# The last chunk's attention due between the preceding chunk's MLP steps, and the block products' bank copies all by ScalarE, ahead of its other work

## The chip, the cores and the metric

The kernel runs on one core of one Trainium2 chip. A core has five engines that run side by side, each taking its own instructions strictly in order: TensorE (PE: matrix products; PEld is its weight load), VectorE (DVE), ScalarE (ACT), GpSimd (POOL) and SyncE (SP), which here issues every DMA. Matrix products land in PSUM banks, which VectorE and ScalarE can read. The metric is the device time of one execution in microseconds, median of three runs.

## The reference, cut to what matters

Attention with a window of 32 positions (half of the heads take every fourth of 128 positions) over 4 batches, 8 heads, 576 positions, head size 64, and then two gated MLPs over the 2304 x 512 result, all in fp32:

```python
x = attn_out.transpose(0, 2, 1, 3).reshape(2304, 512)
xn = x / sqrt(mean(x * x) + 1e-6) * rms_g
x = (silu(xn @ w_gate) * (xn @ w_val)) @ w_out          # 512 -> 1536 -> 512
y = (sigmoid(x @ w2_gate) * (x @ w2_val)) @ w2_out      # 512 -> 1536 -> 512
```

## The kernel before, in words

**Number format.** Every fp32 operand of a product is split into a high and a low half (`split`: the high half by ScalarE or VectorE at L402 or L404, the low half by GpSimd or VectorE at L406 or L409), and a product takes three matmuls: high by high, high by low, low by high. Weights arrive as 64-bit words; `words` turns each block of 128 x 512 of them into fp32 with one ScalarE instruction (L380) and four on VectorE (L386, L389, L392, L395). Such a block is called a word here. `weight_ahead` makes words ahead of time, stores them to DRAM, and the second MLP's 36 words are made so while the first MLP runs. Each word takes one of three SBUF buffers named `wst`, filled by a DMA, and holds it until its L395.

**Stages.** 48 attention groups (`attn_group`: scores L700, masks L711, exponentials L717, transposes L742, values L754, each group a chain through PE, VectorE, ScalarE, VectorE, GpSimd, PE, ScalarE, PE, ScalarE) give the input of six chunks of 384 tokens. `x_norm` takes a chunk's root mean square (squares L798, sums over blocks L806 by GpSimd, over partitions L814 by PE), a Newton iteration on tiny tiles (L848 to L852, GpSimd), spreads and transposes the factor (L855, L870) and writes the split operands `xo`. The first MLP runs over the six chunks twice, with half of its hidden width each time: 72 steps (`mlp_step` and `y_group`), each a gate product (L973, bank g), a value product (L973, bank v), tanh and two multiplications (L985, L987, L991), the split into `h`, and the four output products of the step before it (L1010). Steps 0 to 35 take chunks 0 to 5, six steps each, so chunk 5 begins at step 30, and its `x_norm` must be done by then.

**Second MLP.** It runs over pairs of chunks of 288 tokens in `unit`, with seven block products in place of eight (L1147), sums of blocks being made beforehand (`weight_blocks` L485, `x_blocks` L926, whose seven split operands lie in buffers named xo, wst and xo2). A unit takes the seven products into three banks: X (bank g or v), and Z and Y (both named att). Three times a bank is copied out (`snap`, L1157 on ScalarE or L1159 on VectorE), so that the next product can be added to the same bank or a later result can be made from the copy; VectorE adds the other banks to these copies (`plus`, L1164). There are 24 units of two such halves, 48 x 3 = 144 copies. The next product to a copied bank waits for the copy.

**What sets the order.** All instructions are handed to `Line`, with a cost, a due time and the data they need. `emit` walks a planned clock: on each engine it takes the operation that can start first, and of several that can start at the same time the one with the smallest due time. An operation with `other=` may go to a second engine, which counts as starting later by a penalty of PARAMS. The result is a fixed order on each engine. Due times of attention groups come from pairs lo and hi, on a clock where step k of the first MLP is due at 6.24 k:

```python
lo, hi = PARAMS[f"lo{c}"], PARAMS[f"hi{c}"]
for i, g in enumerate(span):
    due[g] = lo + (hi - lo) * i / len(span)
```

The second MLP's words have a release time on the planned clock (`t + 135` in `whole`), before which `emit` doesn't take them.

Of the kernel before, what the change touches and what calls it, by code (L numbers as in the profile page):

```python
# [23 lines left out]

PARAMS = {
    "margin": 187.0, "wait": 0.344, "w_sq": 2.0, "w_hi": 0.6, "w_lo": 0.6, "x_hi": 0.5, "x_lo": 0.5,
    "h_hi": 0.3, "h_lo": 0.5, "qk": 0.2, "norm": 4.0, "pts": 4.0, "o": 2.0, "snap": 0.4, "ys": 1.0,
    "ts": 1.0, "cross": 0.25, "same": 0.064, "dma_lat": 2.0, "dma_rate": 260e3,
# [3 lines left out]
    "wdue": -7.2, "wslope": 2.65, "wload": -378.6, "wload_step": 37.9,  # L32
    "warm_n": 18, "warm_t": 10.103, "warm_dt": 0.322, "warm_c": 19, "warm_m": 5, "warm_late": 0.218,
    "warm_due": 15.435, "mask_cost": 0.224, "exp_cost": 0.387, "s_cost": 0.8, "o_cost": 0.6,
# [31 lines left out]
class Line:  # L66
# [13 lines left out]
    def add(self, eng, cost, fn, reads=(), writes=(), tiles=(), due=0.0, lat=0.0,  # L80
            release=0.0, until=None, other=(), bus=0.0):

        o = Op()
        o.ways = {eng: (cost, fn, 0.0)}
        if other:
            kind, eng, cost, fn = other
            o.ways[eng] = cost, fn, PARAMS[kind]  # L90
        o.eng, o.tiles, o.due, o.lat = None, list(tiles), due, lat
        o.seq, o.succs, o.end, o.release = len(self.ops), [], None, release
        o.until, o.bus = until, bus
        preds = set()
        for key in reads:
            if key not in self.writer:
                raise KeyError(key)
            preds.add(self.writer[key])
            self.readers.setdefault(key, []).append(o)
        for key in writes:  # L100
            if key in self.writer:
                preds.add(self.writer[key])
            preds.update(self.readers.pop(key, ()))
            self.writer[key] = o
        preds.discard(o)
        o.preds, o.left = preds, len(preds)
        for p in preds:
            p.succs.append(o)
        for t in o.tiles:
            t.users += 1  # L110
        self.ops.append(o)
        return o
# [78 lines left out]
def attention_then_two_gated_mlps(  # L191
# [15 lines left out]
    nc = tc.nc  # L207
# [7 lines left out]
    T = S // 2  # L215
# [58 lines left out]
    def act(n):  # L274
        return 0.17 + n / 1200

    def dve(n):
        return 0.155 + n / 960
# [847 lines left out]
    def unit(p, b, u, at, extra):  # L1126
# [5 lines left out]
        for which in range(2):  # L1132
            uk = (p, b, u, which)
# [3 lines left out]
            ck = {name: ("c", name, uk) for name in c}  # L1137
# [17 lines left out]
            def snap(name, bank, key):  # L1155
                t = c[name]
                add("ACT", act(T), lambda: nc.scalar.copy(out=t.t, in_=bank.t),  # L1157
                    reads=[(key, uk)], writes=[ck[name]], tiles=[bank, t], due=at,
                    other=("snap", "DVE", dve(T), lambda: nc.vector.tensor_copy(  # L1159
                        out=t.t, in_=bank.t)))  # L1160

            def plus(name, bank, key):
                t = c[name]
# [4 lines left out]
            def finish(name):  # L1168
# [3 lines left out]
                if which == 0:  # L1172
# [13 lines left out]
                      ("hs", p, 2 * b + half, f + e), [tk], [], [t], at, "h")  # L1186

            steps = (("X", lambda: snap("11", X, "X")),
                     ("Z", lambda: (plus("11", Z, "Z"), finish("11"))),
                     ("X", lambda: snap("12", X, "X")),  # L1190
                     ("Y", lambda: snap("22", Y, "Y")),
                     ("X", lambda: (plus("22", X, "X"), finish("22"))),
                     ("Y", lambda: (plus("12", Y, "Y"), finish("12"))),
# [207 lines left out]
```

## Time and profile before

| what | before |
|---|---|
| median of 3 runs (lowest to highest) | 1080.74 us (1080.61 to 1081.27) |
| the profiled execution | 1078.51 us, of which 1076.7 us are the span of the trace |
| busy: PE, DVE, ACT, POOL | 1006.9, 695.7, 458.0, 503.7 us |
| mean granted clock of TensorE | 0.969 |
| first MLP's steps 0 to 71 | about 128 to 624 us of the span |
| second MLP | about 628 to 1077 us |

A row of the trace's timeline has the start, the duration, the engine, the line, what is written from what, and in brackets the idle time of that engine just before with the instruction that ended it. The granted clock is 1.00 when TensorE runs at 2.4 GHz and 0.5 when it runs at 1.2 GHz.

### The profile page before, as it was taken

How to read it: one execution, taken by the hardware profiler on the slowest of the kernel's cores; microseconds unless marked ns; L12 is line 12 of the kernel's file. 1: busy time of each engine (PE TensorE's matmuls, PEld its weight loads, DVE VectorE, ACT ScalarE, POOL GpSimd, SP SyncE). 2: the span in 40 equal slices, each digit the busy share in tenths (PEclk: the TensorE clock that was granted, in tenths of full speed). 3: DMA queues.
4: the chain of work that ended last, by engine and by line, in shares of the span. 5: the costliest groups of instructions: out<-in, count | busy, mean ns of one | idle time of the engine just before them, and what ended most of it. 6: DMA issues, size and time to landing. Idle time of an engine off the chain costs nothing.

```text
span 1076.7 us, 20044 instructions
## 1 busy us (share of the span) xinstructions
PE 1006.9 (94%) x7254; PEld 964.7 (90%) x7254; DVE 695.7 (65%) x1479; ACT 458.0 (43%) x1231; POOL 503.7 (47%) x659
## 2 busy tenths in 40 slices
PE   5989699989997799999999988999999999999997
PEld 4768588879996799999999978999999999999996
DVE  3699967686551326777777987647554666466733
ACT  4867655554332233322223344445544344433321
POOL 3476956454322444512213765438553466553511
PEclk8779899999998799999999999999999999999999
DMA  7858468783440635866765641213323332334334
GB/s 159 177 170 180 117 173 189 166 218 107 155 137 30 208 116 190 299 202 212 265 227 176 192 136 44 69 43 102 108 72 126 110 130 86 116 99 105 72 80 89
DMA packets 190899, 152.05 MB, mean 141 GB/s; under 512 B 131376, under 2 KB 163120, under 8 KB 190800
## 3 DMA queue, kind: packets, MB, share of 16 engines
q1 hardware_dynamic: 190800, 150.77, 48.1%
q8 instruction: 57, 0.93, 0.4%
q14 instruction: 42, 0.34, 0.1%
HBM read 103.55 MB, written 47.19 MB: 140 GB/s over the span
## 4 chain that ended last, share of the span: by engine, by line
PE 71%; DVE 12%; DMA 4%; SPq 4%; issue 4%; POOL 3%; ACT 2%; DVEq 0%; POOLq 0%; ACTq 0%
PE y L1010 23%; PE g L973 12%; PE v L973 11%; PE att L1147 9%; PE g L1147 6%; PE v L1147 5%; SPq L612 1%; PE att L700 1%; DVE t L1180 1%; SPq L659 1%; PE att L754 1%; DVE h L404 1%; DVE wz L389 1%; DMA wst<-in_moe_w_val_dram 1%; DVE h L409 1%
## 5 line engine op out<-in xcount | busy, mean ns | idle before, releaser
L1010 PE MATMUL y<-h,wo 128*128 128x288 f32 (+1 forms) x2016 | 369.9, 313 | 2.0 <-POOL h L406 1.0
L1010 PEld LDWEIGHTS y<-h,wo 128*128 128x128 f32 x2016 | 318.5, 188 | 4.6 <-POOL h L406 1.6
L406 POOL TENSOR_TENSOR h<-t,h 128x288 fp32r<-128x288 f32 (+1 forms) x149 | 146.1, 983 | 303.8 <-ACT h L402 238.9
L973 PE MATMUL g<-xo,w 128*128 128x384 f32 x864 | 170.8, 345 | 5.5 <-DVE t L987 2.5
L973 PE MATMUL v<-xo,w 128*128 128x384 f32 x864 | 163.8, 337 | 0.0
L973 PEld LDWEIGHTS g<-xo,w 128*128 128x128 f32 x864 | 154.2, 193 | 10.0 <-DVE t L987 3.2
L973 PEld LDWEIGHTS v<-xo,w 128*128 128x128 f32 x864 | 150.4, 188 | 1.5
L402 ACT CAST h<-t 128x288 fp32r<-128x288 f32 (+1 forms) x140 | 65.6, 471 | 139.7 <-DVE t L991 76.1
L730 POOL TENSOR_SCALAR pr<-pr,rs 128x96 f32<-128x96 f32 x144 | 63.6, 457 | 79.9 <-DVE rs L725 52.3
L1147 PE MATMUL att<-xo,w 128*128 128x288 f32 x576 | 92.7, 296 | 0.8
L985 ACT ACTIVATE t<-g 128x384 f32<-128x384 f32 x72 | 35.4, 491 | 121.8 <-PE g L973 121.7
L1164 DVE TENSOR_TENSOR t<-t,att 128x288 f32<-128x288 f32 x96 | 43.4, 452 | 65.3 <-PE att L1147 61.6
L1147 PEld LDWEIGHTS att<-xo,w 128*128 128x128 f32 x576 | 81.4, 188 | 2.2 <-DVE t L1159 2.2
L987 DVE SCALAR_TENSOR_TENSOR t<-t,g 128x384 f32<-128x384 f32 x72 | 39.7, 551 | 67.2 <-ACT t L985 66.9
L406 POOL TENSOR_TENSOR xo<-xq,xo 128x576 fp32r<-128x576 f32 x36 | 53.9, 1506 | 35.0 <-ACT xo L402 35.0
L392 DVE SCALAR_TENSOR_TENSOR wz<-wst,wz 128x512 int32<-128x512 int32 x72 | 67.7, 940 | 1.4
L1147 PE MATMUL v<-xo,w 128*128 128x288 f32 x396 | 64.1, 297 | 2.9 <-DVE t L1159 2.8
L380 ACT ACTIVATE wz<-wst 128x512 f32<-128x512 f32 x72 | 48.1, 668 | 39.3 <-DMA wst<-in_moe_w_gate_dram 17.4
L717 ACT ACTIVATE pr<-pr,nmx 128x96 f32<-128x96 f32 x144 | 52.6, 367 | 28.5 <-DVE nmx L711 28.3
L1147 PE MATMUL g<-xo,w 128*128 128x288 f32 x396 | 63.2, 295 | 0.0
L991 DVE TENSOR_TENSOR t<-t,v 128x384 f32<-128x384 f32 x72 | 39.6, 550 | 34.0 <-PE v L973 33.5
L395 DVE SCALAR_TENSOR_TENSOR wz<-wst,wz 128x512 int32<-128x512 int32 x72 | 60.5, 840 | 1.5
(170 smaller groups left out, 1597.5 us busy)
## 6 DMA issues: line engine op xcount, KB each, us to landing
z<-wz SPq DMA_DIRECT2D x54, 256.0 KB
wst<-in_moe_w_gate_dram SPq DMA_DIRECT2D x24, 512.0 KB
wst<-in_moe_w_val_dram SPq DMA_DIRECT2D x24, 512.0 KB
wst<-in_moe_w_out_dram SPq DMA_DIRECT2D x24, 512.0 KB
z<-z SPq DMA_DIRECT2D x48, 256.0 KB
xq<-y SPq DMA_DIRECT2D x20, 576.0 KB
x<-xo SPq DMA_DIRECT2D x12, 768.0 KB
xo<-x SPq DMA_DIRECT2D x12, 768.0 KB
```

The costliest lines, as they stand in the source:

```text
L380: add("ACT", act(CW), lambda: nc.scalar.activation(out=z.t.bitcast(F32), in_=top().bitcast(F32), func=ACTF.Square), reads=[("wst", key)], ...
L392: add("DVE", dve(CW), lambda: nc.vector.scalar_tensor_tensor(out=z.t, in0=top(), scalar=-0x40000000, in1=z.t, op0=ALU.bitwise_and, op1=ALU ...
L395: add("DVE", dve(CW), lambda: nc.vector.scalar_tensor_tensor(out=z.t, in0=low(), scalar=29, in1=z.t, op0=ALU.logical_shift_right, op1=ALU. ...
L402: add("ACT", act(n), lambda: nc.scalar.copy(out=hi(), in_=src()), reads=reads, writes=[key] + [order] * bool(order), tiles=tiles + [dst], ...
L406: add("PL", pool(n), lambda: nc.gpsimd.tensor_tensor(out=lo(), in0=src(), in1=hi().bitcast(F32), op=ALU.subtract), reads=reads, writes=[ke ...
L717: add("ACT", PARAMS["exp_cost"], lambda u=u: nc.scalar.activation(out=pr.t[:, u], in_=pr.t[:, u], func=ACTF.Exp, bias=nmx.t[:, u:u + 1], s ...
L730: add("PL", 0.33, lambda u=u: nc.gpsimd.tensor_scalar(out=pr.t[:, u], in0=pr.t[:, u], scalar1=rs.t[:, u:u + 1], scalar2=1.0, op0=ALU.mult, ...
L973: nc.tensor.matmul(out=bank.t, lhsT=w[:, l, cols], rhs=x[:, r, j], start=kk == 0 and n == 0, stop=kk == KD - 1 and n == 2)
L987: add("DVE", dve(T1), lambda: nc.vector.scalar_tensor_tensor(out=t.t, in0=t.t, scalar=1.0, in1=gb.t, op0=ALU.add, op1=ALU.mult), writes=[k ...
L1010: nc.tensor.matmul(out=yb.t, lhsT=w.t[:, l, s], rhs=h.t[:, r], start=n == 0 and j == 0, stop=n == nf - 1 and j == 2)
L1147: nc.tensor.matmul(out=bank.t, lhsT=l.t[:, a, cols], rhs=r.t[:, d, j], start=first and j == 0 and m == 0, stop=j == 1 and m == 2, skip_gro ...
L1164: add("DVE", dve(T), lambda: nc.vector.tensor_tensor(out=t.t, in0=t.t, in1=bank.t, op=ALU.add), reads=[(key, uk)], writes=[ck[name]], tile ...
```

## The change

The span of due times of the last chunk's attention groups goes from 186.7 falling to 113.2, to 80.0 rising to 140.0. The bank copies of `snap` lose their second engine, and their due time falls by 150.

```diff
-    "h_hi": 0.3, "h_lo": 0.5, "qk": 0.2, "norm": 4.0, "pts": 4.0, "o": 2.0, "snap": 0.4, "ys": 1.0,
+    "h_hi": 0.3, "h_lo": 0.5, "qk": 0.2, "norm": 4.0, "pts": 4.0, "o": 2.0, "snap": 150.0, "ys": 1.0,
...
-    "hi4": 108.9, "lo5": 186.7, "hi5": 113.2, "lead": -15.1, "xdue": 7.2,
+    "hi4": 108.9, "lo5": 80.0, "hi5": 140.0, "lead": -15.1, "xdue": 7.2,
...
             def snap(name, bank, key):
                 t = c[name]
                 add("ACT", act(T), lambda: nc.scalar.copy(out=t.t, in_=bank.t),
-                    reads=[(key, uk)], writes=[ck[name]], tiles=[bank, t], due=at,
-                    other=("snap", "DVE", dve(T), lambda: nc.vector.tensor_copy(
-                        out=t.t, in_=bank.t)))
+                    reads=[(key, uk)], writes=[ck[name]], tiles=[bank, t],
+                    due=at - PARAMS["snap"])
```

Three places of the resulting order follow. A row names the line, the operation, the written tile and what is read, and the free size. Lines behind L1159 have one number less in the changed kernel.

**TensorE, steps 28 to 30.** Before, between step 28's output products and step 30's gate product stand the last attention group (L700, L742, L754) and chunk 5's sums (L814) and transpose (L870):

```order
L973 MATMUL g<-xo,w 128x384 x12
L973 MATMUL v<-xo,w 128x384 x12
L1010 MATMUL y_4261<-h,wo 128x384 x3
L1010 MATMUL y_4269<-h,wo 128x384 x3
L1010 MATMUL y_4274<-h,wo 128x384 x3
L1010 MATMUL y_4279<-h,wo 128x384 x3
L700 MATMUL att<-kT,qT 64x96 x6
L742 MATMUL att<-ident,pr 96x128 x3
L754 MATMUL att<-pts,v 64x64 x6
L814 MATMUL att<-ones,pt 128x1 x3
L870 MATMUL att<-ident,rb 128x128 x3
L973 MATMUL g<-xo,w 128x384 x12
```

In the changed kernel the L700 to L754 rows of the last groups stand at steps 15 to 21, L814 behind step 22's value product and L870 among the output products behind step 23's, and at steps 29 and 30 there are MLP products alone. Step 15, which had the scores of two groups before, has those of four in the changed kernel (the row x12 holds two):

```order
L973 MATMUL v<-xo,w 128x384 x12
L754 MATMUL att<-pts,v 64x64 x6
L700 MATMUL att<-kT,qT 64x96 x12
L1010 MATMUL y_3223<-h,wo 128x384 x3
L1010 MATMUL y_3232<-h,wo 128x384 x3
L700 MATMUL att<-kT,qT 64x96 x6
L1010 MATMUL y_3276<-h,wo 128x384 x3
L1010 MATMUL y_3298<-h,wo 128x384 x3
L700 MATMUL att<-kT,qT 64x96 x6
L973 MATMUL g<-xo,w 128x384 x12
L742 MATMUL att<-ident,pr 96x128 x6
```

What moved: nothing of attention or of chunk 5's norm is left ahead of step 30.

**VectorE, from the first MLP's end to the first bank sum of the second MLP.** Before (L485 sums weight blocks, L409 and L404 split, L1033 takes the first MLP's last outputs, L1164 is the first unit's first `plus`):

```order
L485 TENSOR_TENSOR S_7193<-z_7093,z_7144 128x256
L485 TENSOR_TENSOR S_7200<-S_7185,z_7093 128x256
L409 TENSOR_TENSOR xo_7187<-xq_5905,xo_7187 128x576
L409 TENSOR_TENSOR wst_7202<-T3_5968,wst_7202 128x576
L404 CAST wo_7219<-z_7177 128x512
L1033 SCALAR_TENSOR_TENSOR pt_6624<-y0_6902,pt_6624 128x384
L1033 SCALAR_TENSOR_TENSOR pt_6624<-y1_6908,pt_6624 128x384
L1033 SCALAR_TENSOR_TENSOR pt_6624<-y2_6913,pt_6624 128x384
L1033 SCALAR_TENSOR_TENSOR pt_6624<-y3_6922,pt_6624 128x384
L409 TENSOR_TENSOR w_7211<-S_7185,w_7211 128x256
L485 TENSOR_TENSOR S_7257<-z_7093,S_7200 128x256
L1164 TENSOR_TENSOR t_7252<-t_7252,att_7245 128x288
```

In the changed kernel:

```order
L392 SCALAR_TENSOR_TENSOR wz_7182<-wst_7113,wz_7182 128x512
L1033 SCALAR_TENSOR_TENSOR pt_6588<-y0_6866,pt_6588 128x384
L395 SCALAR_TENSOR_TENSOR wz_7182<-wst_7113,wz_7182 128x512
L485 TENSOR_TENSOR S_7245<-z_7066,S_7197 128x256
L386 TENSOR_SCALAR wz_7235<-wz_7235 128x512
L1033 SCALAR_TENSOR_TENSOR pt_6588<-y1_6871,pt_6588 128x384
L389 SCALAR_TENSOR_TENSOR wz_7235<-wst_7170,wz_7235 128x512
L1033 SCALAR_TENSOR_TENSOR pt_6588<-y2_6876,pt_6588 128x384
L392 SCALAR_TENSOR_TENSOR wz_7235<-wst_7170,wz_7235 128x512
L1033 SCALAR_TENSOR_TENSOR pt_6588<-y3_6885,pt_6588 128x384
L395 SCALAR_TENSOR_TENSOR wz_7235<-wst_7170,wz_7235 128x512
L1163 TENSOR_TENSOR t_7233<-t_7233,att_7224 128x288
```

What moved: before, the last word's L395 stands in step 69; in the changed kernel two of the four words behind step 69 are made between the last step's products and the first bank sum. The first unit's sixth and seventh products read the operands wst_7264 and wst_7295, which take over the buffers of wst_7113 and wst_7170.

**VectorE, one later unit.** Before, three copies (L1159) of one half unit stand among the sums (L1164), the gates (L1180) and a split:

```order
L1159 COPY t2_8289<-v_8267 128x288
L1164 TENSOR_TENSOR t2_8289<-t2_8289,att_8282 128x288
L1180 SCALAR_TENSOR_TENSOR t2_8214<-t2_8214,t2_8289 128x288
L404 CAST h2_8322<-t2_8214 128x288
L1159 COPY t2_8324<-v_8267 128x288
L409 TENSOR_TENSOR h2_8322<-t2_8214,h2_8322 128x288
L1159 COPY t2_8340<-att_8315 128x288
L1164 TENSOR_TENSOR t2_8340<-t2_8340,v_8267 128x288
```

In the changed kernel:

```order
L1163 TENSOR_TENSOR t2_8280<-t2_8280,att_8282 128x288
L1179 SCALAR_TENSOR_TENSOR t2_8214<-t2_8214,t2_8280 128x288
L404 CAST h2_8319<-t2_8214 128x288
L409 TENSOR_TENSOR h2_8319<-t2_8214,h2_8319 128x288
L409 TENSOR_TENSOR wst_8324<-xq_8026,wst_8324 128x576
L1163 TENSOR_TENSOR t2_8330<-t2_8330,v_8267 128x288
```

What moved: the copies are all on ScalarE, 144 rows of L1157 where there were 115, and a low half (wst_8324) stands among VectorE's rows.

## Rows read from the trace of the kernel before

**Rows 1.** The page, part 1: busy time, share of the span, instructions.

```profile
PE 1006.9 (94%) x7254; PEld 964.7 (90%) x7254; DVE 695.7 (65%) x1479; ACT 458.0 (43%) x1231; POOL 503.7 (47%) x659
```

**Rows 2.** Five stretches: length, busy time of each engine, PE clock, DMA share, GB/s.

```profile
140.00:335.00 195.00, 189.88 (x1465) 174.79 (x1464) 125.71 (x343) 89.02 (x282) 82.96 (x155) 1.00 0.58 155
335.00:365.00 30.00, 15.63 (x82) 13.05 (x81) 7.74 (x21) 7.11 (x20) 9.88 (x22) 0.66 0.31 103
365.00:620.00 255.00, 253.86 (x1462) 252.90 (x1461) 177.84 (x269) 80.16 (x166) 96.48 (x92) 1.00 0.63 209
620.00:660.00 40.00, 32.44 (x213) 30.24 (x212) 35.54 (x52) 20.02 (x46) 27.81 (x23) 1.00 0.28 90
660.00:1060.00 400.00, 393.77 (x2943) 389.35 (x2942) 238.52 (x442) 167.76 (x399) 195.91 (x193) 1.00 0.31 93
```

**Rows 3.** PE's waits from 335 to 365 us: total, times, longest.

```profile
PE att L870 <- DVE rb L855: 4.7, 1, 4.7
PE att L814 <- POOL pt L806: 4.6, 1, 4.6
```

**Rows 4.** PE's timeline, output products of steps 27, 28 and 29.

```profile
330.93 2.24 PE L1010 MATMUL y<-h,wo 128*128 128x384 f32 x12
...
337.17 2.25 PE L1010 MATMUL y<-h,wo 128*128 128x384 f32 x12
...
365.79 2.24 PE L1010 MATMUL y<-h,wo 128*128 128x384 f32 x12
```

**Rows 5.** PE's timeline, steps that hold parts of attention or norm.

```profile
257.51 2.24 PE L973 MATMUL g<-xo,w 128*128 128x384 f32 x12
...
271.11 2.24 PE L973 MATMUL g<-xo,w 128*128 128x384 f32 x12
...
275.26 2.24 PE L1010 MATMUL y<-h,wo 128*128 128x384 f32 x12
...
289.55 2.35 PE L1010 MATMUL y<-h,wo 128*128 128x384 f32 x12
```

**Rows 6.** PE's waits from 620 to 660 us.

```profile
PE g L1147 <- DVE t L1159: 3.1, 1, 3.1
PE att L1147 <- DVE t L1159: 1.9, 1, 1.9
```

**Rows 7.** PE's waits from 660 to 1060 us.

```profile
PE v L1147 <- DVE t L1159: 4.4, 7, 1.6
...
PE g L1147 <- ACT t L1157: 0.4, 1, 0.4
```

**Rows 8.** The bank copies, largest group of each engine: ns least/median/most, first and last start.

```profile
L1157 ACT COPY t<-g x46: 378/400/402, 629.6 to 1040.6; 128x288 f32<-128x288 f32 x46
...
L1159 DVE COPY t<-v x18: 443/455/459, 638.6 to 1014.7; 128x288 f32<-128x288 f32 x18
```

**Rows 9.** VectorE's instructions of a word, by line: busy us, mean ns.

```profile
L392 DVE SCALAR_TENSOR_TENSOR wz<-wst,wz 128x512 int32<-128x512 int32 x72 | 67.7, 940 | 1.4
L395 DVE SCALAR_TENSOR_TENSOR wz<-wst,wz 128x512 int32<-128x512 int32 x72 | 60.5, 840 | 1.5
L389 DVE SCALAR_TENSOR_TENSOR wz<-wst,wz 128x512 int32<-128x512 int32 x72 | 58.0, 805 | 1.9
...
L386 DVE TENSOR_SCALAR wz<-wz 128x512 f32<-128x512 f32 x72 | 41.9, 582 | 24.9 <-ACT wz L380 24.7
```

**Rows 10.** Timeline at the second MLP's start: last outputs, first bank sum, seventh product.

```profile
623.61 2.42 PE L1010 MATMUL y<-h,wo 128*128 128x384 f32 x13
...
634.20 0.44 DVE L1164 TENSOR_TENSOR t<-t,att 128x288 f32<-128x288 f32 x1
...
636.75 1.05 PE L1147 MATMUL g<-wst,w 128*128 128x288 f32 x6
```

**Rows 11.** Timeline of VectorE, one instruction of a word beside GpSimd's and one apart.

```profile
602.49 1.54 DVE L389 SCALAR_TENSOR_TENSOR wz<-wst,wz 128x512 int32<-128x512 int32 x1
...
613.53 0.69 DVE L389 SCALAR_TENSOR_TENSOR wz<-wst,wz 128x512 int32<-128x512 int32 x1
```

## The prediction, written before the changed kernel ran

> **What bounds the kernel now.** The page's first part comes first: PE is busy for 94% of the span and no other engine for more than 65% [rows 1]. So time can only come from the stretches in which PE stands still or runs at the lower clock. The stretches show them [rows 2]. From 140 to 335 us PE idles 5.1 us, from 365 to 620 us 1.1, from 660 to 1060 us 6.2. From 335 to 365 us it is busy for 15.6 of 30 us, with a granted clock of 0.66, so it spends part of that stretch at 1.2 GHz. From 620 to 660 us it idles 7.6 us while VectorE is busy for 35.5 of 40. The kernel is thus bound by PE except in two places: step 29 of the first MLP, and the start of the second MLP. In the first, the waits name the chain of the last chunk's norm: 4.6 us for GpSimd's sums of squares and 4.7 us for the spread factor behind the Newton iteration [rows 3], each once, with nothing else for PE to do. In the second, VectorE's queue is the cause: the longest waits are for bank copies that stand in it [rows 6]. From 660 us on the same copies cost 4.4 of 6.2 us, seven times [rows 7].
>
> **The hole at step 29.** The change takes attention and norm out of step 29 and puts them between steps 15 and 23. A plain step is 6.24 us, from 330.93 to 337.17; the next output products start at 365.79, so two steps took 34.86 us, 22.38 more than two plain ones [rows 4]. Of this, the PE work of one group, the sums and the transpose moves rather than disappears. Its price at full clock is in two steps with sums and transpose (13.60 us, 1.12 more than plain) and two with a group's three parts (14.29 us, 1.81 more) [rows 5]: 2.93 us. So the hole costs 22.38 - 2.93 = 19.45 us: 14.4 us of idle time [rows 2] and some 5 us of work at half clock. I take all 19.45. What could leave some is that chunk 5's operands come late for another reason. They need the two buffers of chunk 3, free behind step 23, where the order now has the transpose; six steps, 37 us, are then left for the split, more than the whole of the 22.38. If PE idled no more but still lost its clock somewhere, only 14.4 us would be won; that is the lower end.
>
> **Denser attention before it.** Step 15 gets four groups' scores where it had two. The chain of a group runs through four engines, and PE's queue has fixed places for its parts, so each denser place can wait. The whole stretch of 195 us, with about half of the 48 groups, idles 5.1 us [rows 2], or some 0.2 us a group; nine groups have new places, which makes 1.8, and I take 2. The ends are 0 (VectorE is busy for 126 of 195 us there, so there is room) and 5.1 (as much again as the whole stretch).
>
> **The start of the second MLP.** Here the change has a price that its few words don't tell. The second MLP's words have release times on the planned clock, and these don't move, while the first MLP now ends some 19 us or three steps sooner. So in the changed order four words stand behind step 69, where none stood, and two of them between the last step's products and the first bank sum. In the trace of before, that first sum starts 10.6 us after the last value product ended (623.61, where the output products begin), at 634.20, and the first unit's seventh product follows at 636.75 [rows 10]. In the changed order VectorE has there: nine instructions of words, 0.84 for the one left of a word and 2 x 3.17 for two whole ones, 7.2 us at their means [rows 9]; and eleven others, a multiplication, four sums of weight blocks, four output sums, two splits, at 0.68 each, the stretch's mean (35.54 us for 52) [rows 2]: 7.5 us. In the 8.3 us before (one step and a third), it has seven instructions of words (5.5) and six others (4.1), so it comes 1.3 us late. The first sum then starts 16.0 us after the last value product, 5.4 later than before. The seventh product can't be sooner either: its operand wst_7295 takes over the buffer that the last word frees, and needs a cast and a subtraction behind that. So this costs 5.4 us. The cover that hid these words was step 60 to 69's slack on VectorE; there is none here.
>
> The durations are the doubt. The same instruction of a word took 0.69 us when GpSimd stood still and 1.54 when it was subtracting [rows 11]. With the twelve two-input instructions of the four words at 0.69 in place of their mean of 0.86, the cost falls by 2.1 to 3.3; at 1.54 it rises by 8.1 to 13.5. I keep the means, since GpSimd is busy for 28 of 40 us there and not all [rows 2]. The Trainium skill (SBUF — State Buffer, "Who interferes with whom") says that a VectorE instruction with two SBUF inputs and a GpSimd instruction that reads SBUF exclude each other for the whole of an instruction; that speaks against this change, since it puts such instructions where GpSimd splits operands, and would make the 13.5 the sum's term. This case's two rows [rows 11] agree that the length jumps; that each of the twelve would meet one isn't shown.
>
> **The bank copies.** Twenty-nine of 144 copies leave VectorE, the largest group 0.455 us each, for ScalarE, where one takes 0.400 [rows 8]. What counts is the waiting. PE loses 4.4 us from 660 us on [rows 7] and 1.9 at the end of the second unit [rows 6]; the 3.1 at the first unit lies in the 10.6 us above and isn't counted again. The 115 copies that ScalarE makes already cost PE 0.4 us there [rows 7], so 29 more at that rate cost 0.1. That gives 4.4 + 1.9 - 0.1 = 6.2 us, which I take. The ends are 6.3 (all) and 0 (ScalarE's queue is as late as VectorE's was). What stands behind a copy on ScalarE is tanh and casts; ScalarE is busy for 168 of 400 us there [rows 2], which covers a delay of a copy's length. VectorE loses 13 us of work in the second MLP, which is worth nothing by itself since PE bounds it.
>
> Other moved work (stores of chunk 5's operands, loads of the part sums, weights for step 36) keeps its place by step in SP's order within a few steps, and transfers take a third to two thirds of the engines [rows 2]; I cost it at nothing. If that cover failed, PE would wait at step 36.
>
> **The sum.** -19.45 + 2 + 5.4 - 6.2 = -18.25 us. The profiled execution took 1078.51 us, so 1060.3; the median of the runs is 2.2 above it, so 1062.5 us. With the ends: at best -19.45 + 0 + 3.3 - 6.3 = -22.5, or 1058.3; at worst -19.45 + 5.1 + 13.5 + 0 = -0.9, or 1079.9, and 5 more if the clock's part stays.
>
> **Rivals.**
> 1. *The second MLP's start takes more of it back.* With the words at their length beside GpSimd the sum is -19.45 + 2 + 13.5 - 6.2 = -10.2, so 1070.6. For it: rows 11, and VectorE's 35.5 of 40 us before anything is added. Against it: both engines' queues have gaps.
> 2. *The hole moves instead of closing.* Four groups at step 15 share one VectorE queue with words and transposes of loaded heads, and chunk 3's or 4's start then waits. If half of the hole comes back, 9.7 us, the time is 1072. Against it: in the changed order the norms of chunks 3 to 5 stand at least four steps ahead of their first step.
> 3. *Slower: copies first park ScalarE.* Its queue is in order, so a copy placed ahead of tanh and casts holds them until its product is done; gates, the next unit's operands and so PE's products come late. It decides from 18.25/144 = 0.13 us for each copy, on top of the present; at 0.1 it gives 1077, at 0.2 it gives 1091. For it: the copy's due time puts it ahead of everything on ScalarE. Against it: 0.4 us for 115 copies [rows 7], and an engine that is idle for more than half of the stretch.
>
> That the change doesn't do what it says is ruled out for the order, which shows both parts made.
>
> **How the numbers follow.** The forecast, with ends 1056 to 1067, has 0.66; rival 1 (1067 to 1075) 0.17; rival 2 (1068 to 1078) 0.08; rival 3 0.05, of which four parts in five end slower; 0.04 is left for less than 1056, if the other waits of 620 to 660 us go too. The range that leaves out some 2 in 10 is 1056 to 1071. No change that a measurement can tell is within 0.2%, or 2.2 us, of 1080.74; from these cases faster has 0.93, same 0.03, slower 0.04.
>
> **What would show it.** Right: no stretch of 20 us before 600 us with PE below 18 busy and a clock below 1.00, once chunk 1 has begun; step 30 begins 6.3 us after step 29; no L1159 row in the waits; a wait of 5 us or more in all at the first unit's sixth or seventh product, put down to VectorE, or to GpSimd's or ScalarE's split of wst. Wrong: a wait of some us at steps 15 to 17 or 24; PE waiting for L1157 in many places; or no longer a wait at the second MLP's start at all, which would make the sum 5 us too high.

## The result, and the profile after

The changed kernel takes 1064.11 us (median of four runs, 1062.35 to 1066.97), the kernel before beside it 1081.01 (four runs): a ratio of 0.985, interval 0.982 to 0.987, or 16.9 us faster. The forecast was 1062.5. In a second set of six runs the ratio was 0.987 (0.984 to 0.990; 1061.59 to 1070.98 us). One of the six executions of attention alone, below, took 1233 us at a granted clock of 0.74, and the median given there is that of the other five. The profiled execution of the changed kernel is the slowest of its four, with 1066.97 us and a span of 1065.1. So the two profiled executions lie only 11.5 us apart, 5.4 less than the medians, and what the traces show of each term has to add up to 11.6 us of span.

Five stretches of the changed kernel, with the columns of [rows 2], the last three cut some 20 us sooner than there, since the stages begin sooner:

```profile
140.00:335.00 195.00, 189.95 (x1482) 175.06 (x1481) 127.34 (x360) 93.63 (x298) 93.63 (x181) 0.99 0.61 170
335.00:365.00 30.00, 29.41 (x170) 29.09 (x169) 7.48 (x14) 8.12 (x18) 10.19 (x12) 1.00 0.36 123
365.00:600.00 235.00, 233.78 (x1347) 233.14 (x1346) 160.22 (x242) 70.07 (x146) 77.76 (x75) 1.00 0.61 200
600.00:640.00 40.00, 31.05 (x169) 29.32 (x169) 33.29 (x48) 18.52 (x43) 27.29 (x26) 0.83 0.51 170
640.00:1050.00 410.00, 402.11 (x3018) 399.12 (x3017) 252.69 (x456) 177.36 (x431) 195.57 (x188) 1.00 0.30 91
```

The hole of 335 to 365 us is gone: PE is busy for 29.4 of 30 us at a granted clock of 1.00, where it had 15.6 at 0.66. The denser stretch before it idles as much as it did. But the start of the second MLP, from 600 to 640 us, now has a clock of 0.83, where the same stage had 1.00 [rows 2].

To see what each stage gained, the two traces are cut at the same instructions. Before, PE's timeline has these: output products of a step among the attention, the first unit's eighth product (the first of its value side), and the second MLP's first output product.

```profile
137.74 2.35 PE L1010 MATMUL y<-h,wo 128*128 128x384 f32 x12
...
637.65 0.96 PE L1147 MATMUL v<-xo,w 128*128 128x288 f32 x6
...
660.96 0.57 PE L1010 MATMUL y<-h,wo 128*128 128x288 f32 x3
```

After, PE's timeline has the same places, and the two steps that answer to 337.17 and 365.79 in [rows 4]:

```profile
139.50 2.36 PE L1010 MATMUL y<-h,wo 128*128 128x384 f32 x12
...
342.14 2.24 PE L1010 MATMUL y<-h,wo 128*128 128x384 f32 x12
...
348.38 2.24 PE L1010 MATMUL y<-h,wo 128*128 128x384 f32 x12
...
606.94 0.34 PE L1010 MATMUL y<-h,wo 128*128 128x384 f32 x1
...
630.26 1.64 PE L1147 MATMUL v<-xo,w 128*128 128x288 f32 x6
...
653.83 0.57 PE L1010 MATMUL y<-h,wo 128*128 128x288 f32 x3
```

| stage | before, us | after, us | change | forecast |
|---|---|---|---|---|
| up to the first of these rows | 137.74 | 139.50 | +1.76 | 0 |
| to the step ahead of the hole | 199.43 | 202.64 | +3.21 | 2.93 moved + 2 = +4.93 |
| the step with the hole | 28.62 | 6.24 | -22.38 | -22.38 |
| to the last outputs of the first MLP | 257.82 | 258.56 | +0.74 | 0 |
| from there to the eighth product | 14.04 | 23.32 | +9.28 | +5.4 |
| to the second MLP's first output product | 23.31 | 23.57 | +0.26 | -1.8 |
| to the end of the span | 415.74 | 411.27 | -4.47 | -4.4 |

A second profiled execution of the changed kernel, from the second set, has a span of 1064.9 us. Against the same trace of before its changes are, in this order, +0.23, +1.91, -22.38, +1.28, +8.69, and -1.53 for the last two stages together. The order of instructions is the same in both, so stages that differ between them by 1 to 3 us differ by the execution.

The waits of PE from 590 to 660 us say what the second MLP's start waits for now (compare [rows 6]):

```profile
PE y L1010 <- DVE h L409: 3.2, 1, 3.2
PE v L1147 <- DVE t L1163: 3.0, 1, 3.0
PE g L1147 <- ACT wst L402: 1.6, 1, 1.6
```

PE's timeline there shows in what order, and at what speed:

```profile
607.83 2.20 PE L1010 MATMUL y<-h,wo 128*128 128x384 f32 x11 [0.55 <-POOL h L406]
611.48 0.44 PE L1010 MATMUL y<-h,wo 128*128 128x384 f32 x1 [1.44 <-ACT h L402]
615.11 3.89 PE L1010 MATMUL y<-h,wo 128*128 128x384 f32 x11 [3.19 <-DVE h L409]
618.79 1.42 PE L1147 MATMUL g<-xo,w 128*128 128x288 f32 x6
...
624.96 0.92 PE L1147 MATMUL att<-wst,w 128*128 128x288 f32 x5 [1.33 <-POOL wst L406]
627.47 0.58 PE L1147 MATMUL g<-wst,w 128*128 128x288 f32 x1 [1.59 <-ACT wst L402]
628.89 1.57 PE L1147 MATMUL g<-wst,w 128*128 128x288 f32 x5 [0.84 <-POOL wst L406]
```

Eleven matmuls that take 2.20 us at 607.83 take 3.89 at 615.11, behind the waits: TensorE has gone to 1.2 GHz (granted clock 0.50 from 615.2 to 618.7 us), and it does so again at 628.89 (0.50 from 629.0 to 630.4). Between 606.94 and 630.26 PE waits 8.94 us and works 14.38. Before, it waited 3.64 and worked 10.40 in the same stage. So 5.3 us of the 9.28 are waits and 4.0 are longer work. Some 2.8 of the 4.0 are half clock (3.89 for 2.20, 1.42 for 0.96, 1.57 for 0.92); the rest are products that the waits have broken up. This says where PE's time went, and not yet which wait set the length of the stage, since a later wait can take up an earlier one.

VectorE's timeline shows whom the longest wait was for. The last gate's second multiplication (L991) stands between a word's instructions, and the low half of the last `h` behind the split of an operand of the second MLP:

```profile
610.28 0.54 DVE L991 TENSOR_TENSOR t<-t,v 128x384 f32<-128x384 f32 x1
610.75 0.75 DVE L395 SCALAR_TENSOR_TENSOR wz<-wst,wz 128x512 int32<-128x512 int32 x1
611.41 1.97 DVE L409 TENSOR_TENSOR xo<-xq,xo 128x576 fp32r<-128x576 f32 x1
613.30 1.75 DVE L409 TENSOR_TENSOR h<-t,h 128x384 fp32r<-128x384 f32 x1
...
626.52 0.44 DVE L1163 TENSOR_TENSOR t<-t,att 128x288 f32<-128x288 f32 x1
```

The first bank sum comes at 626.52, 19.6 us after the output products begin, where 10.6 was the value before and 16.0 the forecast. It is 9.0 us later, and PE reaches the eighth product 9.28 us later. What joins the two is the last word, in VectorE's and then ScalarE's timeline:

```profile
621.25 0.43 DVE L386 TENSOR_SCALAR wz<-wz 128x512 f32<-128x512 f32 x1 [0.57 <-ACT wz L380]
...
625.85 0.75 DVE L395 SCALAR_TENSOR_TENSOR wz<-wst,wz 128x512 int32<-128x512 int32 x1
```

```profile
626.69 0.67 ACT L402 CAST wst<-xq 128x576 fp32r<-128x576 f32 x1 [2.91 <-DVE wz L395]
```

The cast for the seventh product's operand waits for the last word's L395, PE waits 1.59 us for the cast, and then 0.84 for the low half behind it. VectorE's rows have no gap from 605.97 to that L395 but the 0.57 us at 621.25. So it is VectorE's queue that sets when the eighth product can start, and PE's earlier stops at `h`, with their half clock, are taken up by it. Without them the stage would be shorter by at most some 1.2 us: the 0.57, and 0.65 for the product at 628.89. In the second execution, and in the run below whose copies are not ahead, PE stops at `h` for the same 3.2 us and VectorE has no gap at all; the stage is 22.73 and 22.20 us long.

From 660 to 1045 us no wait for a copy on VectorE is left, against 4.4 us in [rows 7], but one for bank sums has come:

```profile
PE v L1147 <- DVE t L1163: 2.8, 2, 2.0
...
PE g L1147 <- ACT t L1157: 0.3, 2, 0.2
```

### The profile page after: what moved, and what is told of

It reads as the page before. It is cut to its first block, busy times and chain, and to the rows that moved or that the text cites. A ratio compares the mean times of both kernels' runs of the same rounds, so it can differ in the third digit from the quotient of the medians.

```text
span 1065.1 us, 20056 instructions
## 1 busy us (share of the span) xinstructions
PE 1006.3 (94%) x7254; PEld 968.6 (91%) x7254; DVE 689.1 (65%) x1465; ACT 460.6 (43%) x1253; POOL 494.6 (46%) x651
## 4 chain that ended last, share of the span: by engine, by line
PE 71%; DVE 12%; issue 5%; POOL 3%; DMA 3%; ACT 3%; SPq 2%; DVEq 0%; ACTq 0%; POOLq 0%
PE y L1010 23%; PE g L973 12%; PE v L973 11%; PE att L1147 9%; PE g L1147 6%; PE v L1147 6%; PE att L700 2%; DVE wz L389 1%; DVE t L1179 1%; PE att L754 1%; DVE S L485 1%; DMA wst<-in_moe_w_val_dram 1%; SPq L537 1%; DVE wz L392 1%; DVE wz L395 1%
## 5 line engine op out<-in xcount | busy, mean ns | idle before, releaser
L1010 PE MATMUL y<-h,wo 128*128 128x288 f32 (+1 forms) x2016 | 374.3, 315 | 7.4 <-DVE h L409 3.2
L1010 PEld LDWEIGHTS y<-h,wo 128*128 128x128 f32 x2016 | 320.7, 189 | 11.5 <-DVE h L409 3.4
L406 POOL TENSOR_TENSOR h<-t,h 128x288 fp32r<-128x288 f32 (+1 forms) x146 | 140.4, 965 | 319.8 <-ACT h L402 268.9
L973 PE MATMUL g<-xo,w 128*128 128x384 f32 x864 | 168.1, 342 | 4.0 <-DVE t L987 3.1
L402 ACT CAST h<-t 128x384 fp32r<-128x384 f32 (+1 forms) x138 | 64.9, 473 | 159.0 <-DVE t L991 95.6
L1163 DVE TENSOR_TENSOR t<-t,att 128x288 f32<-128x288 f32 x96 | 43.2, 450 | 74.0 <-PE att L1147 73.6
L406 POOL TENSOR_TENSOR xo<-xq,xo 128x576 fp32r<-128x576 f32 x31 | 49.9, 1615 | 35.6 <-ACT xo L402 33.1
L392 DVE SCALAR_TENSOR_TENSOR wz<-wst,wz 128x512 int32<-128x512 int32 x72 | 63.0, 875 | 1.4
L380 ACT ACTIVATE wz<-wst 128x512 f32<-128x512 f32 x72 | 47.9, 666 | 32.5 <-DMA wst<-in_moe_w_gate_dram 12.0
L991 DVE TENSOR_TENSOR t<-t,v 128x384 f32<-128x384 f32 x72 | 39.5, 549 | 34.7 <-PE v L973 34.2
L389 DVE SCALAR_TENSOR_TENSOR wz<-wst,wz 128x512 int32<-128x512 int32 x72 | 60.6, 842 | 1.8
```

Source lines behind the costliest of these rows:

```text
L380: add("ACT", act(CW), lambda: nc.scalar.activation(out=z.t.bitcast(F32), in_=top().bitcast(F32), func=ACTF.Square), reads=[("wst", key)], ...
L389: add("DVE", dve(CW), lambda: nc.vector.scalar_tensor_tensor(out=z.t, in0=top(), scalar=3, in1=z.t, op0=ALU.logical_shift_left, op1=ALU.bi ...
L392: add("DVE", dve(CW), lambda: nc.vector.scalar_tensor_tensor(out=z.t, in0=top(), scalar=-0x40000000, in1=z.t, op0=ALU.bitwise_and, op1=ALU ...
L402: add("ACT", act(n), lambda: nc.scalar.copy(out=hi(), in_=src()), reads=reads, writes=[key] + [order] * bool(order), tiles=tiles + [dst], ...
L406: add("PL", pool(n), lambda: nc.gpsimd.tensor_tensor(out=lo(), in0=src(), in1=hi().bitcast(F32), op=ALU.subtract), reads=reads, writes=[ke ...
L973: nc.tensor.matmul(out=bank.t, lhsT=w[:, l, cols], rhs=x[:, r, j], start=kk == 0 and n == 0, stop=kk == KD - 1 and n == 2)
```

## The experiments

**The two parts apart.** The attention's due times alone:

```diff
-    "hi4": 108.9, "lo5": 186.7, "hi5": 113.2, "lead": -15.1, "xdue": 7.2,
+    "hi4": 108.9, "lo5": 80.0, "hi5": 140.0, "lead": -15.1, "xdue": 7.2,
```

> The attention's new due times alone; the bank copies stay as before, on ScalarE or VectorE. Theory A (the four terms add up as in the prediction): 1081.0 - 19.45 + 2 + 5.4, so about 1069, with 1159 waits of about 4 us still there behind the second MLP's start. Theory B (the copies' part gave little of the result, since waits for the sums of L1163 took the place of the waits for copies): 1064 to 1066, as the whole change. If the start of the second MLP costs 8 instead of 5.4, as the trace of the changed kernel suggests, theory A's figure is 1071.6.

Measured: 1068.73 us, ratio 0.990 (0.988 to 0.992). The same kernel once more:

> The attention's new due times alone, once more, for its profile and for a second time beside the others on this chip: 1067 to 1071 as measured; waits for copies of L1159 or L1157 of about 4 us from 660 us on.

Measured: 1069.88, ratio 0.990 (0.987 to 0.993). Its waits from 660 us on hold the copies as expected:

```profile
PE v L1147 <- DVE t L1159: 4.5, 7, 1.6
```

From the last outputs to the eighth product it takes 22.16 us, against 14.04 before: the dearer start belongs to the attention's part, with no help from the copies. The copies alone:

```diff
-    "hi4": 108.9, "lo5": 80.0, "hi5": 140.0, "lead": -15.1, "xdue": 7.2,
+    "hi4": 108.9, "lo5": 186.7, "hi5": 113.2, "lead": -15.1, "xdue": 7.2,
```

(as a change of the changed kernel).

> The bank copies alone, all by ScalarE and ahead of its other work; the attention's due times stay as before, so the hole at step 29 stays open. Theory A: 1081.0 - 6.2, so about 1074.8, and no wait for a copy that stands on VectorE. Theory B: waits for bank sums on VectorE (3.2 us in the changed kernel) take most of it back: 1077 to 1080.

Measured: 1073.82, ratio 0.9945 (0.9925 to 0.9964), 5.9 us faster by the ratio and 4.8 by the medians. Theory A holds, and theory B falls in both runs: the parts give some 11 and 6 us, and together the 16.9 measured, within the intervals.

**Is it ScalarE, or being ahead?** The changed kernel, with the copies due with their product:

```diff
-    "h_hi": 0.3, "h_lo": 0.5, "qk": 0.2, "norm": 4.0, "pts": 4.0, "o": 2.0, "snap": 150.0, "ys": 1.0,
+    "h_hi": 0.3, "h_lo": 0.5, "qk": 0.2, "norm": 4.0, "pts": 4.0, "o": 2.0, "snap": 0.0, "ys": 1.0,
```

> The changed kernel with the copies all on ScalarE, but due with their product and not 150 us ahead. Theory A (what counts is that a copy doesn't stand in VectorE's queue): as the changed kernel within 2 us, 1062 to 1066. Rival (what counts is that a copy goes ahead of ScalarE's tanh and casts): waits for copies on ScalarE of 4 us or more behind the second MLP's start, and 1067 to 1071.

Measured: 1068.46, ratio 0.990 (0.988 to 0.992), no faster than the attention's part alone. The rival holds. PE's waits from 660 us on name the copies still, on ScalarE now:

```profile
PE v L1147 <- ACT t L1157: 5.2, 5, 1.3
```

Taking the copies from VectorE was worth nothing by itself; putting them ahead of ScalarE's other work was worth all of their gain. Whether the same lead would do as much with VectorE still open to them was not tried.

**The words at the second MLP's start.** The changed kernel, with their release on the planned clock moved back by the time that the first MLP gained:

```diff
-            weight_ahead(p, f, i, t - 8, t, t + 135)
+            weight_ahead(p, f, i, t - 8, t, t + 115)
```

> The changed kernel with the second MLP's words released 20 us sooner on the planned clock (135 becomes 115), so that the last word stands 21 instructions ahead of the first bank sum on VectorE, as in the kernel before. Theory A (words that stand on VectorE between the last step's products and the first bank sum give back 5.4 to 8 us): the first bank sum comes some 10 to 11 us after the output products begin, the clock stays at 1.00 from 600 us on, and the time is 1056 to 1059. Rival: the start of the second MLP is late for another reason (the splits of h and of the first unit's operands), or the words then disturb steps 50 to 65 as much: 1063 to 1066.

Measured: 1055.55 (1055.38 to 1056.86), ratio 0.9785 (0.9764 to 0.9805), just below theory A's range. The output products begin at 604.08 in its trace, the first bank sum comes 11.1 us later, and the clock from 600 to 640 us is 1.00. Its PE's timeline:

```profile
607.59 2.18 PE L1010 MATMUL y<-h,wo 128*128 128x384 f32 x11 [1.05 <-POOL h L406]
...
616.38 1.07 PE L1147 MATMUL g<-wst,w 128*128 128x288 f32 x6 [3.42 <-ACT t L1157]
...
618.96 0.96 PE L1147 MATMUL v<-xo,w 128*128 128x288 f32 x6
```

From 604.08 to the eighth product at 618.96 it takes 14.88 us, 8.4 less than the changed kernel, and nearly the 14.04 of before. The changed kernel on the same chip, for the difference:

> The changed kernel itself, so that the versions with moved words are compared with it on one chip. Theory and rival: 1062 to 1067, as measured; it is here for the difference.

Measured: 1065.47, ratio 0.987 (0.984 to 0.990). The control, the same edit of the words in the kernel before:

> The kernel before with the same edit to the words alone (135 becomes 115). Theory A (the words cost only because the first MLP now ends sooner; before, none stood behind step 69): as the kernel before within 2 us. Rival (words sooner are worth something by themselves at the second MLP's start): 3 to 6 us faster than before.

Measured: 1080.19, ratio 1.000 (0.999 to 1.002). The words cost nothing in the whole where they were (moved, the stage to the eighth product is 1.9 us shorter and what follows 3.8 longer); what made them dear is that the first MLP now ends sooner.

**The words' length, or the order?** The edit above also changes who splits what. Released 10 us sooner:

```diff
-            weight_ahead(p, f, i, t - 8, t, t + 135)
+            weight_ahead(p, f, i, t - 8, t, t + 125)
```

> The changed kernel with the second MLP's words released 10 us sooner on the planned clock (135 becomes 125): one word instead of three stands on VectorE among the last step's gates, and none behind them. Theory A (each word there costs about its own 3 us): 2 to 4 us above the version with 20 us, so 1057 to 1060. Rival (the price is all in the drop of the clock that the waits bring, which comes or doesn't): within 1 us of one of the two, 1055 to 1057 or 1063 to 1066.

Measured: 1060.64, ratio 0.9825 (0.980 to 0.985), neither the one nor the other. Behind the last gate's multiplication only one instruction of a word is left there, and yet PE waits longer, by its timeline:

```profile
615.46 3.89 PE L1010 MATMUL y<-h,wo 128*128 128x384 f32 x11 [7.11 <-DVE h L409]
```

VectorE's timeline has three block sums (L485) in 4.7 us and two splits ahead of that low half:

```profile
607.84 3.16 DVE L485 TENSOR_TENSOR S<-z 128x256 f32<-128x256 f32 x2
610.92 1.61 DVE L485 TENSOR_TENSOR S<-S,z 128x256 f32<-128x256 f32 x1
612.46 0.74 DVE L409 TENSOR_TENSOR wst<-T,wst 128x576 fp32r<-128x576 f32 x1
613.13 1.28 DVE L409 TENSOR_TENSOR wst<-xq,wst 128x576 fp32r<-128x576 f32 x1
614.33 1.07 DVE L409 TENSOR_TENSOR h<-t,h 128x384 fp32r<-128x384 f32 x1
```

Here the low half of `h` sets the start, and no word. So the words' length was tried by itself: the words at their places, but short. Of the last three words, the four VectorE instructions take 32 of 512 columns:

```diff
-            weight_ahead(p, f, i, t - 8, t, t + 135)
+            weight_ahead(p, f, i, t - 8, t, t + 135, CW if n < len(todo) - 3 else 32)
...
-            out=z.t, in0=top(), scalar=3, in1=z.t, op0=ALU.logical_shift_left,
+            out=z.t[:, :cols], in0=top()[:, :cols], scalar=3, in1=z.t[:, :cols], op0=ALU.logical_shift_left,
```

> The changed kernel in its own order, but the last three words' sixteen-fold shorter on VectorE: their four instructions take 32 of 512 columns, so the rest of these three weight slices stays unrounded. Nothing else moves, neither the release times nor an instruction's place. Theory A (the length of these words on VectorE, 11.1 us in the changed kernel behind the start of the output products, is what the second MLP's start gives back): the first bank sum comes 10 to 13 us after the output products begin instead of 19.6, and the time is 1055 to 1059. Rival (the price lies in the order, where the low half of h stands behind the splits of the first unit's operands and these take long beside GpSimd): 1061 to 1065.

Measured: 1063.74 (1059.12 to 1067.87), ratio 0.984 (0.981 to 0.987); the intervals of this and of the changed kernel overlap. The twelve instructions take 5.35 us in place of 11.10, and the first bank sum comes 16.2 us after the output products begin. But PE still waits 2.8 us for the low half of `h`, and its clock falls as before. Theory A fails: 2.9 us of the stage go, where 5.75 went from VectorE's work. Behind the words stands a second chain that is nearly as long. VectorE is idle for 2.18 us at 617.55, waiting for the last word's L380. On ScalarE this L380 stands behind the first bank copy, the copy waits for PE's first product, and that product comes behind the wait for the low half of `h`. The whole time says less, since this execution also loses some 6 us behind the eighth product (table below). The words don't get as short as their columns, either. VectorE's timeline of this run:

```profile
607.45 2.02 DVE L409 TENSOR_TENSOR xo<-xq,xo 128x576 fp32r<-128x576 f32 x1
...
612.39 0.19 DVE L389 SCALAR_TENSOR_TENSOR wz<-wst,wz 128x32 int32<-128x32 int32 x1
...
617.55 0.18 DVE L386 TENSOR_SCALAR wz<-wz 128x32 f32<-128x32 f32 x1 [2.18 <-ACT wz L380]
...
619.89 0.98 DVE L395 SCALAR_TENSOR_TENSOR wz<-wst,wz 128x32 int32<-128x32 int32 x1
```

and GpSimd's, beside the last of these:

```profile
619.42 1.40 POOL L406 TENSOR_TENSOR wst<-xq,wst 128x576 fp32r<-128x576 f32 x1
```

A two-input instruction on 32 columns takes 0.19 us at 612.39, where GpSimd is idle until 612.99. It takes 0.98 at 619.89, and ends as GpSimd's subtraction ends, at 620.8. Not each one is held: the L389 at 618.11, which starts with a subtraction of GpSimd's, takes 0.18. The Trainium skill (SBUF — State Buffer, "Who interferes with whom") says that a VectorE instruction with two inputs in SBUF contends with a GpSimd instruction that reads SBUF; this pair of rows agrees. In line with it, VectorE's split of an `xo` takes 2.02 us here, at the same time as GpSimd's own, and 0.75 in the version with 20 us.

**Both chains at once.** Released 30 us sooner, the last `h` has its cast and its low half on VectorE directly behind its gate:

```diff
-            weight_ahead(p, f, i, t - 8, t, t + 135)
+            weight_ahead(p, f, i, t - 8, t, t + 105)
```

> The changed kernel with the words released 30 us sooner (135 becomes 105). On VectorE no word stands among the last two steps' gates, and the last step's cast and low half of h stand right behind its gate, with no split of a first unit's operand between. Theory (what counts at the start of the second MLP is when the two halves of the last h come, whether words or splits stand ahead of them): PE waits less than 1.5 us for h there, the clock stays near 1.00, and the time is 1052 to 1056. Rival (words 30 us sooner crowd the steps before, and the first bank sum is late behind the split of wst on VectorE): 1057 to 1061.

Measured: 1052.98 (1051.52 to 1056.18), ratio 0.974 (0.972 to 0.977), the fastest of all. VectorE's and PE's timelines:

```profile
606.12 0.56 DVE L991 TENSOR_TENSOR t<-t,v 128x384 f32<-128x384 f32 x1 [0.60 <-PE v L973]
606.71 0.78 DVE L404 CAST h<-t 128x384 fp32r<-128x384 f32 x1
607.52 1.67 DVE L409 TENSOR_TENSOR h<-t,h 128x384 fp32r<-128x384 f32 x1
```

```profile
609.24 2.18 PE L1010 MATMUL y<-h,wo 128*128 128x384 f32 x11 [0.90 <-DVE h L409]
...
617.11 0.96 PE L1147 MATMUL v<-xo,w 128*128 128x288 f32 x6
```

PE waits 0.9 us there, and reaches the eighth product 11.19 us after 605.92, where the outputs begin: 2.9 us less than before. The expected wait, clock and time came.

**Two attempts to go further** on the version with 20 us. The bank sums ahead, like the copies:

```diff
                     out=t.t, in0=t.t, in1=bank.t, op=ALU.add), reads=[(key, uk)],
-                    writes=[ck[name]], tiles=[bank, t], due=at)
+                    writes=[ck[name]], tiles=[bank, t], due=at - PARAMS["snap"])
```

> The version with words 20 us sooner, and the bank sums on VectorE put ahead of its other work in the same way as the copies. Theory (what empties a bank that a product waits for goes ahead of what only prepares later units): the waits for L1163, 4.9 us from 600 us on in that version, fall below 1.5 us, and the time falls by 3 to 4 us, to 1051 to 1053. Rival (a sum put ahead holds back the splits behind it, and the waits move to them): 1055 to 1058.

Measured: 1057.56 (1056.18 to 1058.22), ratio 0.979 (0.977 to 0.981). From 590 us on the waits for L1163 are 6.3 us instead of 5.2, so the theory falls: a lead in due time isn't what these sums lack. The sums of the first unit's weight blocks sooner:

```diff
-                            weight_blocks(p, f0 + 2 * u, i, at - 24 + 8 * i)
+                            weight_blocks(p, f0 + 2 * u, i, at - 24 + 8 * i - 20 * (p == ONE and u == 0))
```

> The version with words 20 us sooner, and the sums of the first unit's weight blocks due 20 us sooner too. Theory (in that version PE's 3.4 us wait at the first unit's fifth product comes from such a sum, which ScalarE's cast ahead of the copy waits for): that wait falls below 1 us, and the time is 1052 to 1053. Rival (VectorE is full there, so another of its instructions is late instead): 1055 to 1058.

Measured: 1055.90 (1052.38 to 1058.76), ratio 0.976 (0.973 to 0.979). The 3.4 us wait is gone, but PE waits 2.2 us for the low half of `h` and 2.3 for a bank sum instead: the rival's 1055 to 1058.

The stages of the second MLP in these traces, by the same cuts as above:

| kernel | last outputs to eighth product, us | eighth product to the end of the span |
|---|---|---|
| before | 14.04 | 439.05 |
| before, words 20 us sooner | 12.18 | 442.88 |
| copies only | 16.76 | 433.13 |
| attention only | 22.16 | 440.34 |
| changed, copies not ahead | 22.20 | 439.90 |
| changed, two executions | 23.32, 22.73 | 434.84, 437.52 |
| changed, last words short | 20.39 | 441.00 |
| changed, words 10, 20, 30 us sooner | 21.40, 14.88, 11.19 | 434.18, 434.24, 434.39 |
| words 20 us sooner, bank sums ahead | 16.81 | 435.57 |
| words 20 us sooner, first sums sooner | 14.26 | 434.79 |

The first column is long where the attention has moved and the words have not, or have by 10 us only, whatever the copies do. The 16.76 of the copies alone and the 16.81 with bank sums ahead have half clock behind a wait of 3.4 us. The second column is 433.1 to 437.5 where the copies are ahead and 439.1 to 442.9 where they are not; the one with short words stands out because PE waits 1.8 and 4.2 us at 636.93 and 650.11 and runs at half clock behind each.

## Why the prediction was right, step by step

- **The hole at step 29**: -22.38 us in the step itself, as computed, of which 2.93 were to come back as moved work. Right. Step 30 begins 6.24 us after step 29.
- **Denser attention**: 2 us were taken; the stage grew by 3.21, of which the moved work is 2.93, so 0.3 is left. In the second execution the stage grew by 1.91, and in six traces of the other versions with the attention moved it takes 201.8 to 203.5 us. So the term is between some -1 and 1.1 us and was too large: the new places did not cost PE the stretch's mean idle time. The prediction counts nine new places and doesn't say which; the change gives new due times to the four groups of the last chunk's span.
- **The start of the second MLP**: the place and the cause of its being late (words that keep their release while the first MLP ends sooner) are shown by the words' edits, which take 9 to 13 us off the changed kernel, by the ratios, and nothing off the kernel before. The size, 5.4, was too small; it is 9.28 (8.69 in the second execution), and this is the term of the sum that was furthest off. The step it rests on, that PE loses what the first bank sum on VectorE is late, holds: 9.0 us. So does the reason that the seventh product can't be sooner, the buffer of the last word. What was mis-sized is VectorE's queue. The last gate's second multiplication starts 3.3 us after the output products begin and not 1.3, and from there to the sum it takes 16.2 us and not 14.7. The two splits, of `xo` and `h`, take 1.97 and 1.75 us, where 0.68 was taken for each. What the prediction did not see is the second chain, the low half of the last `h` in the same queue, and the half clock behind its wait. In the changed kernel both are taken up by the words, but for some 1.2 us; they show when the words are short or 10 us sooner (2.9 and 1.9 us of the stage go), and only an order that shortens both chains gives back nearly all of the 9.28, or more. That the forecast lateness (5.4) and the measured growth of waits (5.3) agree is chance, since they are different things. The prediction's sign for this step, 5 us of waits at the sixth and seventh product, was 3.76, since PE had done part of its waiting at `h`. And the reading of [rows 11] is not quite right: GpSimd does not stand still through the instruction of 0.69 us, as a subtraction of its starts at 613.83, 0.4 us before that instruction ends.
- **The bank copies**: -6.2 was taken; -4.2 came in this execution, and -1.5 in the second, where the clock falls behind the same waits. The 4.4 from the first output products on came as computed (4.47) in the first. The 1.9 at the second unit's end did not: a bank sum is now late there, 3.0 us at 652.13. The reason was half wrong. The prediction counted the copies' leaving VectorE's queue; the run with copies on ScalarE but not ahead shows 5.2 us of waits for them and no gain. The lower end, "ScalarE's queue is as late as VectorE's was", is what happens without the lead.
- **Rivals**: the first, in which the start takes more back, holds in part: 9.3 lies between 5.4 and its 13.5. The hole did not move. Of the third, copies that park ScalarE, there is one small case: at 620.25 ScalarE has waited 2.29 us for the product of the first copy, with the last word's L380 behind it in the queue, and VectorE stands idle for 0.57 us until that L380 is done. PE waits for no copy longer than 0.6 us in the changed kernel.
- **What lies outside the steps**: +1.76 us ahead of all places that the prediction speaks of. In the traces with the attention moved this first row starts anywhere from 135.65 to 139.50 us (137.74 before), so that is the execution and not the change. Then +0.74 between step 30 and the end of the first MLP (1.28 in the second execution), which the prediction has at nothing. With them the sum is -11.6, where the medians say -16.9. In which stage a typical run of the changed kernel is the 5.4 us better, the traces don't show. The two terms that are shown to be off, 3.9 us at the start of the second MLP and 2.0 at the copies, err to the same side. So it is in part luck that the forecast of 1062.5 lies 1.6 us from the median.

## What to carry to other kernels

When a change makes one stage end sooner, look for all that is held to a time and not to a place: here 36 weight blocks kept their release, met the next stage's start, and took back half of what closing the hole had won, and a shift of that one constant brought another 11 us. Of several waits in a row, ask which one ends last: the 3.2 us at `h` were taken up by the words here, and with the words 10 us sooner the low half of `h` was the wait that counted, at 7.1 us. So at a hand-over between stages follow the last operand of the old stage as well as the first of the new one. And when an operation empties a bank that the busiest engine waits for, its rank in its queue can count more than which engine does it: so it was for the copies, while the bank sums gained nothing by the same lead.

## What the runs showed of the hardware that was not expected

- TensorE fell to half clock behind waits of a few us. After waits of 0.55, 1.44 and 3.19 us within 8 us of 606.94 the next eleven matmuls took 3.89 us in place of 2.20, and three more waits brought products of six matmuls of 1.64 us in place of 0.96. But the same wait doesn't always do so. The version with 20 us waits 3.42 us at 616.38 and goes on at full clock (1.07 us for six matmuls, above); the one with bank sums ahead waits 3.39 at the same product and doesn't, by its PE's timeline:

```profile
615.94 1.81 PE L1147 MATMUL g<-wst,w 128*128 128x288 f32 x6 [3.39 <-ACT t L1157]
```

  It is so between two executions of one kernel, too. The changed kernel's two traces have the same wait at the same product of a later unit. In the first, PE's clock stays at 1.00; in the second it is 0.56 from 793.6 to 796.5 us:

```profile
794.22 1.07 PE L1147 MATMUL v<-xo,w 128*128 128x288 f32 x6 [1.99 <-DVE t L1163]
...
795.93 0.96 PE L1147 MATMUL g<-xo,w 128*128 128x288 f32 x6
```

```profile
792.66 1.06 PE L1147 MATMUL v<-xo,w 128*128 128x288 f32 x6 [1.98 <-DVE t L1163]
...
794.65 1.65 PE L1147 MATMUL g<-xo,w 128*128 128x288 f32 x6
```

  What decides between the two is left open.
- Two executions of one order with nearly the same span (1065.1 and 1064.9 us) differ inside. At 60 to 80 us the clock was 0.91 in one and 0.74 in the other, and the output products that begin at 139.50 in the one began at 137.97 in the other. A change of 1 to 2 us that one trace shows in one stage is no finding by itself.
